# A transformer block on one Trainium2 core: LayerNorm 1 of all blocks by TensorE transposes, warm-up matmuls, early attention for block 0, and exact buffer dependencies

## The chip, the cores and the metric

The kernel runs on one core of a Trainium2 chip. The time is the device time of one execution, in microseconds (us). Before the change it is 264.82 us, the median of 3 runs (264.09 to 265.74).

Names used below, with what this kernel uses each for: TensorE (PE) does the matmuls, VectorE (DVE) and ScalarE (ACT) the elementwise work, GpSimd (POOL) elementwise work too, and SyncE (SP) issues DMA transfers. PSUM buffers hold matmul results until ACT or DVE takes ("evacuates") them to SBUF.

## The reference

One block of a diffusion-style transformer on x of 2048 tokens by 448 channels, in bfloat16: 16 heads of 28 channels, each token attending to itself and to 7 earlier tokens at distance 2, 4, ... 14; a gated MLP of width 1792. Six vectors (shift, scale and gate for each half) come from `silu(c) @ w_mod`.

```python
mod = (_silu(c) @ w_mod).reshape(1, 6, 1, -1)
sa, ca, ga, sb, cb, gb = (mod[:, i] for i in range(6))          # shortened
h = _layernorm(x) * (1 + ca) + sa                               # "LN1"
x = x + ga * attention(h, A_wqkv, A_wo)                         # window 8, dilation 2
h = _layernorm(x) * (1 + cb) + sb                               # "LN2"
gate = h @ W_gate; up = h @ W_up
x = x + gb * ((relu(gate) * up) @ W_down)
```

## The kernel before

The program handles the tokens in 4 blocks of 512 (each 4 tiles of 128) and attention in 18 tiles of up to 114 tokens. It lists all operations with what they read (`r`), what they write (`w`), a priority (`prio`, lower is earlier) and a guess of their cost. A list scheduler then fixes one order for each engine, so a priority or a dependency can move many instructions. A buffer in `w` means: wait for all earlier users of it.

The stages of block b: LN1 gives hT (normalized input, channels on partitions); the Q/K projections (`stage_qk`) and V projections (`stage_v`) read hT; attention tiles (logits, exp, mask, attention times V, division by the sum) give the attention output; the output projection `stage_y` adds it to x; LN2 gives h2T; then gate, up and down matmuls.

LN1 had two forms. Blocks 0 and 1 use TensorE transposes, blocks 2 and 3 DMA transposes with everything else on POOL:

```python
def stage_a_pe(b, prio, groups):
    ...                                             # statistics, 1/sigma
    pairs = [_Buf(poolF) for _ in range(2)]         # PSUM
    for j in range(4):
        hbuf = ln_normalize(..., DVE if b == 0 else POOL)
        ...  # 4 transposes of 128x128 into pairs
    for cc in range(4):
        ...  # evacuate to hT with scale (1+ca) and shift sa: ACT for cc < 2, else DVE

def stage_a_dma(b, prio):
    ...                                             # statistics, 1/sigma
    for t in range(4 * b, 4 * b + 4):
        hbuf = ln_normalize(t, rstd, nmr, 1, prio, POOL)
        ln_transpose(hbuf, ...)                     # DMA transpose into hT
    for cc in range(4):
        ln_affine(...)                              # POOL: hT * (1+ca) + sa, in place
```

Attention of one tile is in two halves that share the buffer `ea`. Both the exp and the mask list the whole of `ea` as written, so the second exp waits for the first mask:

```python
op(ACTE, _act(8 * nq), ex, r=[buf], w=[ea, (ea, half)], prio=eprio)
...
op(DVE, _dve(8 * nq, 0.52), mk, r=[(ea, half), mname], w=[ea, (ea, half, "m")], prio=eprio)
```

In the down-projection each token tile takes a token buffer `tok`, which the output addition also reads. The next tile's matmuls so wait for this tile's addition:

```python
op(PE, 7 * _mm(D), mm, r=..., w=[buf, tok], prio=prio, drain=PE_DRAIN)
...
op(DVE, 620, lambda e: e.tensor_tensor(o.at, buf.at[:, 0:D], x_sb[:, t, :], ALU.add),
   r=[buf, tok, ("x", t)], w=[o], prio=eprio)
```

The end of the program's listing, where the order is set:

```python
mod_cols((0, 1), "wmodA", 0, -5)
stage_a_pe(0, 0, ((0, 2), (2, 4)))
stage_qk(0, 50)
stage_a_pe(1, 30, ((0, 4),))
...                                  # Wg, Wu, Wd loads, issued from POOL, held back
stage_a_dma(2, 60)
stage_a_dma(3, 70)
...                                  # scalings of wo and Wd by the gates, on POOL
for t in range(NA):
    first = t < 5
    stage_attn(t, 200 + t if first else 500 + 10 * t, 140 + t if first else 500 + 10 * t)
    ...                              # stage_y at the same priorities, LN2 after each 4
```

The first priority of `stage_attn` is that of its TensorE work, the second that of ACT and DVE. The projections of block 1 have 150, those of blocks 2 and 3 have 300 and 400.

The softmax here doesn't subtract the row's maximum and nothing guards it: scores larger than these inputs give would overflow.

## Time and profile before

| | before |
|---|---|
| time, median of 3 (range) | 264.82 us (264.09 to 265.74) |
| span of the profiled execution | 262.4 us |
| TensorE busy | 229.6 us, 88% |
| POOL busy | 73.5 us, 28% |
| chain of waits | PE 76%, DVE 11%, POOL 6% |
| first gate matmul | 88.59 us |
| first gate matmul to the end | 173.8 us |

TensorE is the busiest engine and heads the chain of waits (the chain of work that ended last, followed back). The kernel's time is so its matmuls plus the stretches in which TensorE waits or runs slowly. The page of the kernel before, in 40 slices of 6.56 us, gives the busy share in tenths; PEclk is the granted TensorE clock in tenths of full speed:

```profile
PE   0589995468899799999999999999999999999784
...
POOL 7306907998924000013502215020130000000000
PEclk9999999558999999999999999999999999999999
```

The dip of PE in slices 7 to 9 comes with a POOL that is 70% to over 90% busy, and within it, in slices 8 and 9, the granted clock falls to a half. The same stretches with numbers, again for the kernel before (window, its length, PE busy with its instruction count, granted clock, DMA share, GB/s):

```profile
14.00:24.00 10.00, 9.69 (x36) 1.00 1.00 247
...
40.00:60.00 20.00, 10.95 (x138) 0.67 0.40 56
```

From 40 to 60 us TensorE loses 9 us, in part of the rest at half clock. The chain of waits of the kernel before tells why (start, duration, engine, tile and line):

```profile
51.89 2.97 POOL Wd L771 x3
54.87 3.89 POOL hT L510 x4
58.75 1.01 POOL Wd L771
60.05 1.11 PE psF L570 x3
```

L510 is `ln_affine`, L771 the scaling of Wd and L570 the Q/K projections. The projections wait for block 2's LN1, which stands in POOL's queue among other work. (They don't read Wd: the chain names its scaling last only because it ended just before them.)

Two other losses, from the timeline of the kernel before (start, duration, engine, line, operation, result and operands, shape, count, and in brackets the idle time before and what ended it). L597 is the V projection, L736 the down-projection:

```profile
14.09 1.67 PE L597 MATMUL psF<-Wv,hT 128*128 128x448 bf16 x4 [1.61 <-DVE hT L540]
15.98 4.37 PE L570 MATMUL psF<-hT,Wqk 128*128 128x512 bf16 x11 [0.22 <-DVE st L479]
...
88.59 0.81 PE L716 MATMUL psF<-h2T,Wg 128*128 128x512 bf16 x3 [0.16 <-issue]
...
252.77 2.82 PE L736 MATMUL psM<-Wd,bigR 128*128 128x448 bf16 x14 [0.72 <-DVE o_sb L743]
```

The first projections take 0.40 us per matmul, nearly twice what the same matmuls take later (0.22 us): they run "cold", at half rate, until 19.76 us. The recorded clock reads 1.00 from 14 to 24 us all the same, so here the durations decide. At the end, three down-projections (the last is shown) wait 0.72 us each for the output addition (L743). The first gate matmul (L716) at 88.59 us divides the kernel: from then on TensorE waits little, and from 160 to 240 us it is busy over 99%. In the same trace block 0's last output projection starts at 72.71 us, and block 0's h2T is complete at 85.19.

### The profile page before, as it was taken

To read this page: it belongs to the slowest core of one execution; us is meant where nothing else is said; L and a number is where in the kernel's file an instruction comes from. 1 tells how busy PE (TensorE), PEld (TensorE's weight loads), DVE (VectorE), ACT (ScalarE), POOL (GpSimd) and SP (SyncE) were. 2 spreads that over 40 slices of the span, in tenths; PEclk is the share of its full clock that TensorE was granted. 3 is DMA by queue.
4 is the path that set the end of the run, shared out by engine and by line. 5 is a ranking of instruction groups with operands and counts; after the bars stand their busy time and mean duration, and the time that the engine had idled before them with its cause. 6 is when DMAs were issued, how large, how long until landed. Compare 5 with 4: busy or idle time off the path is not lost.

```text
span 262.4 us, 4091 instructions
## 1 busy us (share of the span) xinstructions
PE 229.6 (88%) x1609; PEld 109.4 (42%) x1634; DVE 140.9 (54%) x277; ACT 120.2 (46%) x207; POOL 73.5 (28%) x98
## 2 busy tenths in 40 slices
PE   0589995468899799999999999999999999999784
PEld 0435542123344344444444444444444444444331
DVE  5986506667640377876867889633333433244311
ACT  2237777447547766677575656531113311123100
POOL 7306907998924000013502215020130000000000
PEclk9999999558999999999999999999999999999999
DMA  6996999001001000022002120002100001000011
GB/s 170 290 291 151 339 349 165 20 20 22 20 20 23 0 0 2 0 42 41 20 17 50 28 42 1 0 19 61 37 20 17 0 0 35 21 17 0 0 37 36
DMA packets 20924, 15.92 MB, mean 61 GB/s; under 512 B 13752, under 2 KB 19656, under 8 KB 20904
## 3 DMA queue, kind: packets, MB, share of 16 engines
q1 hardware_dynamic: 19736, 10.61, 17.3%
q0 software_dynamic: 896, 4.82, 5.3%
q8 instruction: 13, 0.21, 0.3%
q10 hardware_dynamic: 272, 0.23, 0.3%
q14 instruction: 7, 0.06, 0.1%
HBM read 10.67 MB, written 1.84 MB: 48 GB/s over the span
## 4 chain that ended last, share of the span: by engine, by line
PE 76%; DVE 11%; POOL 6%; issue 3%; ACT 2%
PE psF L716 36%; PE psM L736 16%; PE psF L570 11%; PE psF L597 4%; PE psM L681 3%; POOL Wd L771 3%; PE psL L624 3%; DVE EA L643 2%; PE psM L652 2%; DVE st L479 1%; POOL hT L510 1%; DVE o_sb L743 1%; ACT EA L638 1%; POOL wo_pad L768 1%; DVE qT L670 1%
## 5 line engine op out<-in xcount | busy, mean ns | idle before, releaser
L722 ACT ACTIVATE g_sb<-psF 128x512 bf16<-128x512 f32 x56 | 33.4, 597 | 67.3 <-PE psF L716 67.2
L724 DVE TENSOR_TENSOR bigR<-psF,g_sb 128x512 bf16<-128x512 f32 x56 | 38.7, 690 | 43.2 <-PE psF L716 39.4
L716 PE MATMUL psF<-h2T,Wu 128*128 128x512 bf16 x215 | 55.9, 379 | 0.8 <-issue 0.5
L716 PE MATMUL psF<-h2T,Wg 128*128 128x512 bf16 x213 | 55.7, 379 | 1.0 <-issue 0.6
L736 PE MATMUL psM<-Wd,bigR 128*128 128x448 bf16 x224 | 47.1, 353 | 3.6 <-DVE o_sb L743 2.6
L497 POOL TENSOR_SCALAR hb<-x_sb,rstd,nmr 128x448 bf16<-128x448 bf16 x28 | 22.4, 810 | 76.1 <-DVE nmr L490 64.0
L638 ACT ACTIVATE EA<-psL 128x912 bf16<-128x912 f32 (+1 forms) x36 | 33.2, 923 | 19.0 <-PE psL L624 16.4
L643 DVE TENSOR_TENSOR EA<-EA,maskA 128x912 bf16<-128x912 bf16 (+1 forms) x36 | 27.3, 758 | 18.5 <-ACT EA L638 18.3
L716 PEld LDWEIGHTS psF<-h2T,Wu 128*128 128x128 bf16 x224 | 21.3, 98 | 24.9
L736 PEld LDWEIGHTS psM<-Wd,bigR 128*128 128x128 bf16 x224 | 21.0, 98 | 25.6 <-DVE o_sb L743 4.0
L570 PE MATMUL psF<-hT,Wqk 128*128 128x512 bf16 x123 | 30.3, 400 | 0.8 <-POOL Wd L771 0.3
L716 PEld LDWEIGHTS psF<-h2T,Wg 128*128 128x128 bf16 x224 | 21.0, 98 | 23.8
L743 DVE TENSOR_TENSOR o_sb<-psM,x_sb 128x448 bf16<-128x448 f32 x16 | 10.0, 624 | 25.8 <-PE psM L736 25.6
L510 POOL TENSOR_SCALAR h2T<-h2T,modc 128x512 bf16<-128x512 bf16 (+1 forms) x16 | 13.7, 856 | 32.3 <-DMA h2T<-hb 31.1
L681 PE MATMUL psM<-wo_pad,qT 128*128 128x448 bf16 x64 | 16.3, 380 | 5.8 <-DVE qT L670 5.8
L479 DVE BATCH_NORM_STATS2 st<-x_sb 128x6 f32<-128x448 bf16 x32 | 19.6, 613 | 0.6
L570 PEld LDWEIGHTS psF<-hT,Wqk 128*128 128x128 bf16 x128 | 12.9, 103 | 16.3 <-issue 3.4
L624 PE MATMUL psL<-qT,kT 28*128 28x114 bf16 (+1 forms) x288 | 14.3, 220 | 4.7 <-ACT EA L638 4.6
L597 PE MATMUL psF<-Wv,hT 128*128 128x448 bf16 (+1 forms) x72 | 15.7, 365 | 1.6 <-DVE hT L540 1.6
L624 PEld LDWEIGHTS psL<-qT,kT 28*128 28x128 bf16 (+1 forms) x288 | 8.3, 98 | 16.9 <-ACT EA L638 7.4
L771 POOL TENSOR_TENSOR Wd<-Wd,gbc 128x448 bf16<-128x448 bf16 x14 | 14.6, 1067 | 0.0
L665 ACT ACTIVATE lnD<-psM 128x456 f32<-128x456 f32 x18 | 9.9, 550 | 7.6 <-PE psM L660 7.6
(70 smaller groups left out, 172.4 us busy)
## 6 DMA issues: line engine op xcount, KB each, us to landing
out_dram<-o_sb SPq DMA_DIRECT2D x16, 112.0 KB, 1.7
bigR<-in_w_mod_dram SPq DMA_DIRECT2D x1, 1568.0 KB, 15.6
Wd<-in_B_W_down_dram POOLq DMA_DIRECT2D x1, 1568.0 KB, 14.1
x_sb<-in_A_x_dram SPq DMA_DIRECT2D x3, 448.0 KB, 9.3
Wg<-in_B_W_gate_dram POOLq DMA_DIRECT2D x1, 1344.0 KB, 6.6
Wu<-in_B_W_up_dram POOLq DMA_DIRECT2D x1, 1344.0 KB, 10.0
bigR<-in_w_mod_dram SPq DMA_DIRECT2D x1, 784.0 KB, 7.5
bigR<-in_A_wqkv_dram SPq DMA_DIRECT2D x1, 672.0 KB, 8.9
```

Source lines behind the costliest of these rows:

```text
L497: f = lambda e: e.tensor_scalar(buf.at[:, 0:D], x_sb[:, t, :], rt[:, t:t + 1], nt[:, t:t + 1], ALU.mult, ALU.add)
L570: last = e.matmul(buf.at, Wqk[:, k, 512 * sec + 128 * g:512 * sec + 128 * g + 128], hT[:, k, KOFF + TB * b:KOFF + TB * b + TB], start=(k = ...
L597: last = e.matmul(buf.at[0:nk, 0:D], hT[:, k, KOFF + k0:KOFF + k0 + nk], Wv[:, k, :], start=(k == 0), stop=(k == 3))
L624: last = e.matmul(buf.at[0:nk, i, g * NQ:g * NQ + nq], kT[32 * r:32 * r + DH, g, KOFF + k0:KOFF + k0 + nk], qT[32 * r:32 * r + DH, g, s0:s ...
L638: return e.activation(dst, src, ACT.Exp)
L643: return e.tensor_tensor(d, d, msk[0:nk, None, 0:nq].to_broadcast([nk, 8, nq]), ALU.mult)
L681: last = e.matmul(buf.at[:, 0:D], qT[:, g, s0:s0 + 128], wo_pad[:, g, :], start=(g == 0), stop=(g == 3))
L716: last = e.matmul(buf.at, W[:, k, 128 * f:128 * f + 128], h2.at[:, k, :], start=(k == 0), stop=(k == 3))
L722: op(ACTE, _act(TB), lambda e, gs=gs, gb=bufs[0]: e.activation(gs.at, gb.at, ACT.Relu), r=[bufs[0]], w=[gs], prio=eprio)
L724: op(DVE, _dve(TB), lambda e, gs=gs, ub=bufs[1], f=f: e.tensor_tensor(hh.at[:, f, :], ub.at, gs.at, ALU.mult), r=[bufs[1], gs], w=[hh, (hh ...
L736: last = e.matmul(buf.at[:, 0:D], hh.at[:, f, 128 * j:128 * j + 128], Wd[:, f, :], start=(f == 0), stop=(f == NF - 1))
L771: op(POOL, 1000, lambda e, f=f: e.tensor_tensor(Wd[:, f, :], Wd[:, f, :], gbc[:, 1, :], ALU.mult), r=[("Wd", f), ("gbc", 1)], w=[("Wds", f ...
```

## The change

It has five intents: (1) take LN1 of blocks 2 and 3 from POOL and the DMA queue to TensorE transposes; (2) keep TensorE's clock up before the first real work by matmuls on zeros; (3) run attention of tiles 0 to 4 (block 0) among the projections of blocks 1 to 3, by TensorE priority 140 in place of 200; (4) drop the two superfluous waits shown above; (5) split and reorder loads, so that all weights are issued early from SP. The diff, cut to its core:

```diff
+        def keep_busy(n, prio, cost):
+            buf = _Buf(poolF)
+            ...   # n matmuls of warm[128x128] by warm[128x512]
+        op(DVE, 150, lambda e: e.memset(warm[:], 0.0), w=["warm"], prio=-30)
+        keep_busy(10, -30, 430)
+        keep_busy(16, -29, 217)
...
-        load(wmod[0:112, :, 0:2 * D], wmod_v[:, :, 0:2 * D], ["wmodA"], D * 2 * D * 2, -8)
+        load(wmod[0:112, 0:2, 0:2 * D], wmod_v[:, 0:2, 0:2 * D], ["wmodA0"], D * D * 2, -8)
+        load(wmod[0:112, 2:4, 0:2 * D], wmod_v[:, 2:4, 0:2 * D], ["wmodA1"], D * D * 2, -8)
...                # mod_cols: two halves, each after its half of the weights
+        for W, src, n in ((Wg, B_W_gate, "Wg"), (Wu, B_W_up, "Wu")):
+            load(...)                                  # from SP
+        load(Wd[:], ...)                               # from SP
...
-                op(ACTE, _act(8 * nq), ex, r=[buf], w=[ea, (ea, half)], prio=eprio)
+                op(ACTE, _act(8 * nq), ex, r=[buf] + ([ea] if half else []), w=[(ea, half)] + ([] if half else [ea]),
+                   prio=eprio)
...
-                op(DVE, ..., mk, r=[(ea, half), mname], w=[ea, (ea, half, "m")], prio=eprio)
+                op(DVE, ..., mk, r=[ea, (ea, half), mname], w=[(ea, half, "m")], prio=eprio)
...
-                   r=[buf, tok, ("x", t)], w=[o], prio=eprio)
+                   r=[buf, ("x", t)], w=[o], prio=eprio)
...
         stage_a_pe(0, 0, ((0, 2), (2, 4)))
+        keep_busy(5, 1, 217)
         stage_qk(0, 50)
         stage_a_pe(1, 30, ((0, 4),))
-        ...       # Wg, Wu, Wd loads from POOL
-        stage_a_dma(2, 60)
-        stage_a_dma(3, 70)
+        stage_a_pe(2, 60, ((0, 4),))
+        stage_a_pe(3, 70, ((0, 4),))
...
-            stage_attn(t, 200 + t if first else 500 + 10 * t, 140 + t if first else 500 + 10 * t)
+            stage_attn(t, 140 + t if first else 500 + 10 * t, 140 + t if first else 500 + 10 * t)
...                # stage_y likewise
```

The change also stops the scheduler from giving one buffer twice to one operation, and adds a DVE memset of hT's unused rows for blocks 2 and 3 (`hT1`). It also moves the second set of modulation vectors from priorities 230 to 232 to 136 to 139; makes the dependencies on h2T exact, like those on `ea`; and alters a few cost guesses.

More of the change, by code (lines that the diff above doesn't have):

```diff
@@ L114, in lat, with slot_for @@
             return self.XLAT
-        def slot_for(buf):
+        def slot_for(buf, taken=()):
             s = buf.slots
@@ L119, in slot_for @@
             for i, prev in enumerate(s.last):
+                if (id(s), i) in taken:
+                    continue
                 if prev is None:
@@ L135, in schedule @@
                 bad = False
+                taken = set()
                 for b in o["allocs"]:
-                    s = slot_for(b)
+                    s = slot_for(b, taken)
                     if s is None:
@@ L140, in schedule @@
                         break
+                    taken.add((id(b.slots), s[1]))
                     slot_t = max(slot_t, s[0])
@@ L333, in bass_adaLN_cond__sliding_local_dilated__glu_gated_reglu__prompt_kernel @@
         nmr2 = sb("nmr2", [128, NT], F32)
+        warm = sb("warm", [128, 512], BF16)
         crow = sb("crow", [112, 4], BF16)
@@ L373, in bass_adaLN_cond__sliding_local_dilated__glu_gated_reglu__prompt_kernel @@
         op(DVE, 350, lambda e: e.memset(hT[64:128, 3, KOFF:KOFF + 2 * TB], 0.0), w=["hT0"], prio=-14)
+        op(DVE, 350, lambda e: e.memset(hT[64:128, 3, KOFF + 2 * TB:KOFF + S], 0.0), w=["hT1"], prio=26)
         op(DVE, 350, lambda e: e.memset(Wqk[64:128, 3, :], 0.0), w=["wqkz"], prio=-14)
@@ L394, in bass_adaLN_cond__sliding_local_dilated__glu_gated_reglu__prompt_kernel, with mm @@
            r=["Bsel"], w=["Bsel"], prio=-8)
+        def keep_busy(n, prio, cost):
+            buf = _Buf(poolF)
+            def mm(e):
+                last = None
+                for _ in range(n):
+                    last = e.matmul(buf.at, warm[:, 0:128], warm[:, 0:512], start=True, stop=True)
+                return last
+            op(PE, n * cost, mm, r=["warm"], w=[buf], prio=prio, drain=PE_DRAIN)
+        op(DVE, 150, lambda e: e.memset(warm[:], 0.0), w=["warm"], prio=-30)
+        keep_busy(10, -30, 430)
+        keep_busy(16, -29, 217)
         def load(dst, src, w, nbytes, prio, r=(), eng=SP, issue=450.0):
@@ L408, in bass_adaLN_cond__sliding_local_dilated__glu_gated_reglu__prompt_kernel @@
         load_x(2, 4, -9, eng=ACTE)
-        load(wmod[0:112, :, 0:2 * D], wmod_v[:, :, 0:2 * D], ["wmodA"], D * 2 * D * 2, -8)
+        load(wmod[0:112, 0:2, 0:2 * D], wmod_v[:, 0:2, 0:2 * D], ["wmodA0"], D * D * 2, -8)
+        load(wmod[0:112, 2:4, 0:2 * D], wmod_v[:, 2:4, 0:2 * D], ["wmodA1"], D * D * 2, -8)
+        load(Wv[:, 0:3, :], A_wqkv[0:384, 2 * D:3 * D].rearrange("(k p) n -> p k n", p=128),
+             [("wv", k) for k in range(3)], 384 * D * 2, -7)
+        load(Wv[0:64, 3, :], A_wqkv[384:448, 2 * D:3 * D], [("wv", 3)], 64 * D * 2, -7)
         load(Wraw[:, 0:3, :], A_wqkv[0:384, 0:2 * D].rearrange("(k p) n -> p k n", p=128),
@@ L412, in bass_adaLN_cond__sliding_local_dilated__glu_gated_reglu__prompt_kernel @@
         load(Wraw[0:64, 3, :], A_wqkv[384:448, 0:2 * D], [("wraw", 3)], 64 * 2 * D * 2, -7)
-        load(Wv[:, 0:3, :], A_wqkv[0:384, 2 * D:3 * D].rearrange("(k p) n -> p k n", p=128),
-             [("wv", k) for k in range(3)], 384 * D * 2, -7)
-        load(Wv[0:64, 3, :], A_wqkv[384:448, 2 * D:3 * D], [("wv", 3)], 64 * D * 2, -7)
         load_x(4, 8, -6)
         load_x(8, 12, -5)
-        load_x(12, 16, -5)
-        load(wmod[0:112, :, 2 * D:6 * D], wmod_v[:, :, 2 * D:6 * D], ["wmodB"], D * 4 * D * 2, -4)
+        load(wmod[0:112, 0:2, 2 * D:6 * D], wmod_v[:, 0:2, 2 * D:6 * D], ["wmodB0"], D * 2 * D * 2, -4)
+        load(wmod[0:112, 2:4, 2 * D:6 * D], wmod_v[:, 2:4, 2 * D:6 * D], ["wmodB1"], D * 2 * D * 2, -4)
+        load_x(12, 16, -4)
         for r in range(4):
@@ L422, in bass_adaLN_cond__sliding_local_dilated__glu_gated_reglu__prompt_kernel @@
                  [("wo", r)], 4 * DH * D * 2, -3, r=["wo0"])
+        for W, src, n in ((Wg, B_W_gate, "Wg"), (Wu, B_W_up, "Wu")):
+            load(W[:, 0:3, :], src[0:384, :].rearrange("(k p) n -> p k n", p=128), [n + "a"], 384 * FF * 2, -2)
+            load(W[0:64, 3, :], src[384:448, :], [n + "b"], 64 * FF * 2, -2)
+        load(Wd[:], B_W_down.rearrange("(f p) n -> p f n", p=128), [("Wd", f) for f in range(NF)], FF * D * 2, -1)
         op(POOL, 900, lambda e: e.memset(Wqk_h[:, :, :, DH:32], 0.0), r=["wqkz"], w=["wqk0"], prio=-16)
@@ L441, in mod_cols, with mm @@
             buf = _Buf(poolM)
-            def mm(e):
+            def mm(e, ks):
                 last = None
-                first = True
-                for vi, vec in enumerate(vecs):
+                for k in ks:
                     for cc in range(4):
-                        for k in range(4):
+                        for vi, vec in enumerate(vecs):
                             M = ROWS[cc]
@@ L451, in mm @@
                                             wmod[0:112, k, D * vec + 128 * cc:D * vec + 128 * cc + M],
-                                            silu[:, k:k + 1], start=first, stop=(vi == 1 and cc == 3 and k == 3),
+                                            silu[:, k:k + 1], start=(k == 0 and cc == 0 and vi == 0),
+                                            stop=(k == 3 and cc == 3 and vi == 1),
                                             skip_group_check=True)
-                            first = False
                 return last
             op(DVE, 70, lambda e: e.memset(buf.at[:, 0:8], 0.0), w=[buf], prio=prio - 20)
-            op(PE, 2400, mm, r=[wname, "silu"], w=[buf], prio=prio, drain=PE_DRAIN)
-            op(DVE, 150, lambda e: e.tensor_copy(modc[:, col:col + 4], buf.at[:, 0:4]), r=[buf, "eps"],
+            for i in range(2):
+                op(PE, 750, lambda e, i=i: mm(e, (2 * i, 2 * i + 1)), r=[wname + str(i), "silu"], w=[buf], prio=prio,
+                   drain=PE_DRAIN)
+            op(DVE, 80, lambda e: e.tensor_copy(modc[:, col:col + 4], buf.at[:, 0:4]), r=[buf, "eps"],
                w=[("mod", col)], prio=prio)
@@ L471, in mm @@
                 return last
-            op(PE, 4 * _mm(D), mm, r=["wmodB", "silu_bc"], w=[buf], prio=prio, drain=PE_DRAIN)
+            op(PE, 4 * _mm(D), mm, r=["wmodB0", "wmodB1", "silu_bc"], w=[buf], prio=prio, drain=PE_DRAIN)
             op(((ACTE, _act(D), lambda e: e.activation(gbc[:, i, :], buf.at[:, 0:D], ACT.Copy)),
@@ L485, in ln_rstd @@
             ts = range(t0, t1)
-            op(ACTE, 290, lambda e: e.activation(lt[:, t0:t1], mvt[:, t0:t1, 1], ACT.Ln, bias=eps_col[:, 0:1]),
+            op(ACTE, 300, lambda e: e.activation(lt[:, t0:t1], mvt[:, t0:t1, 1], ACT.Ln, bias=eps_col[:, 0:1]),
                r=[(tag, "mv", t) for t in ts] + ["eps"], w=[(tag, "ln", t0)], prio=prio)
@@ L493, in ln_rstd, with ln_normalize @@
                w=[(tag, "nmr", t) for t in ts], prio=prio)
-        def ln_normalize(t, rt, nt, tag, prio, eng):
+        def ln_normalize(t, rt, nt, tag, prio, eng, extra=()):
             buf = _Buf(hb_slots)
@@ L498, in ln_normalize, with ln_transpose @@
                                           ALU.mult, ALU.add)
-            op(eng, 390 if eng == DVE else 620, f, r=[("x", t), (tag, "rstd", t), (tag, "nmr", t)], w=[buf],
+            op(eng, 390 if eng == DVE else 720, f, r=[("x", t), (tag, "rstd", t), (tag, "nmr", t)], w=[buf] + list(extra),
                prio=prio)
             return buf
-        def ln_transpose(buf, dst, w, prio):
-            op(SP, 0, lambda e: e.dma_start_transpose(dst(), buf.at), r=[buf], w=w, prio=prio, dma=450000,
+        def ln_transpose(buf, dst, r, w, prio):
+            op(SP, 0, lambda e: e.dma_start_transpose(dst(), buf.at), r=[buf] + r, w=w, prio=prio, dma=20000,
                issue=1250.0)
@@ L511, in f @@
                                        modc[0:rows, col + cc:col + cc + 1], ALU.mult, ALU.add)
-            op(POOL, 700, f, r=deps + [("mod", col), ("mod", col + 4)], w=w, prio=prio)
+            op(POOL, 850, f, r=deps + [("mod", col), ("mod", col + 4)], w=w, prio=prio)
         def stage_a_pe(b, prio, groups):
@@ L540, in stage_a_pe @@
                 fd = lambda e, src=src, dst=dst, sc=sc, bi=bi: e.tensor_scalar(dst, src(), sc, bi, ALU.mult, ALU.add)
-                op(*((ACTE, 720, fa) if cc < 2 else (DVE, 700, fd)), r=pairs[cc // 2:cc // 2 + 1] + [("mod", 0), ("mod", 4), "hT0"],
+                op(*((ACTE, 720, fa) if cc < 2 else (DVE, 700, fd)), r=pairs[cc // 2:cc // 2 + 1] + [("mod", 0), ("mod", 4)],
                    w=[("hT", b, cc)], prio=prio)
-        def stage_a_dma(b, prio):
-            for t in range(4 * b, 4 * b + 4):
-                ln_stats(t, st, mv, 1, prio)
-            ln_rstd(4 * b, 4 * b + 4, mv, lnv, rstd, nmr, 1, prio)
-            for t in range(4 * b, 4 * b + 4):
-                hbuf = ln_normalize(t, rstd, nmr, 1, prio, POOL)
-                c0 = KOFF + 128 * t
-                ln_transpose(hbuf, lambda c0=c0: hT[:, :, c0:c0 + 128], [("hTr", t)], prio)
-            for cc in range(4):
-                R = ROWS[cc]
-                ln_affine(lambda cc=cc, R=R, b=b: hT[0:R, cc, KOFF + TB * b:KOFF + TB * b + TB],
-                          [("hTr", t) for t in range(4 * b, 4 * b + 4)], [("hT", b, cc)], 0, R, cc, prio)
         qscale = float(DH) ** -0.5
@@ L572, in mm @@
                         return last
-                    op(PE, 4 * _mm(TB), mm, r=[("wqk", k, sec) for k in range(4)] + ["wqkz", "hT0"] + hT_deps(TB * b, TB * b + TB),
+                    op(PE, 4 * _mm(TB), mm, r=[("wqk", k, sec) for k in range(4)] + ["wqkz", "hT0"] + (["hT1"] if b > 1 else []) + hT_deps(TB * b, TB * b + TB),
                        w=[buf], prio=prio, drain=PE_DRAIN)
@@ L599, in mm @@
                 return last
-            op(PE, 4 * _mm(D), mm, r=[("wv", k) for k in range(4)] + ["wvz", "hT0"] + hT_deps(k0, k0 + nk) + (["hTpad"] if t == 0 else []),
+            op(PE, 4 * _mm(D), mm, r=[("wv", k) for k in range(4)] + ["wvz", "hT0"] + (["hT1"] if k0 + nk > 2 * TB else []) + hT_deps(k0, k0 + nk) + (["hTpad"] if t == 0 else []),
                w=[buf], prio=prio, drain=PE_DRAIN)
@@ L643, in mk @@
                     return e.tensor_tensor(d, d, msk[0:nk, None, 0:nq].to_broadcast([nk, 8, nq]), ALU.mult)
-                op(DVE, _dve(8 * nq, 0.52), mk, r=[(ea, half), mname], w=[ea, (ea, half, "m")], prio=eprio)
+                op(DVE, _dve(8 * nq, 0.52), mk, r=[ea, (ea, half), mname], w=[(ea, half, "m")], prio=eprio)
             ob = _Buf(poolM)
@@ L693, in stage_ln2 @@
                 for j in (j0, j0 + 1):
-                    hbuf = ln_normalize(j, rstd2, nmr2, 2, prio, POOL)
+                    hbuf = ln_normalize(j, rstd2, nmr2, 2, prio, POOL, [h2] if j == 4 * b else [])
                     c0 = 128 * (j - 4 * b)
-                    ln_transpose(hbuf, lambda c0=c0: h2.at[:, :, c0:c0 + 128], [h2, (h2, "r", j)], prio)
+                    ln_transpose(hbuf, lambda c0=c0: h2.at[:, :, c0:c0 + 128], [h2], [(h2, "r", j)], prio)
             for cc in range(4):
                 R = ROWS[cc]
-                ln_affine(lambda cc=cc, R=R: h2.at[0:R, cc, :], [(h2, "r", j) for j in range(4 * b, 4 * b + 4)],
-                          [h2, (h2, cc)], 8, R, cc, prio)
+                ln_affine(lambda cc=cc, R=R: h2.at[0:R, cc, :], [h2] + [(h2, "r", j) for j in range(4 * b, 4 * b + 4)],
+                          [(h2, cc)], 8, R, cc, prio)
             return h2
@@ L705, in stage_gu @@
             hh = _Buf(hh_slots)
-            extra = ["wmodA", "wmodB"] + [("wraw", k) for k in range(4)]
+            extra = ["wmodA0", "wmodA1", "wmodB0", "wmodB1"] + [("wraw", k) for k in range(4)]
             for f in range(NF):
@@ L750, in bass_adaLN_cond__sliding_local_dilated__glu_gated_reglu__prompt_kernel @@
         stage_a_pe(0, 0, ((0, 2), (2, 4)))
+        keep_busy(5, 1, 217)
         stage_qk(0, 50)
         stage_a_pe(1, 30, ((0, 4),))
-        hold = [("x", 12), (1, "nmr", 7)]
-        load(Wg[:, 0:3, :], B_W_gate[0:384, :].rearrange("(k p) n -> p k n", p=128), ["Wga"], 384 * FF * 2, 45,
-             eng=POOL, issue=1100.0, r=hold)
-        load(Wg[0:64, 3, :], B_W_gate[384:448, :], ["Wgb"], 64 * FF * 2, 45, eng=POOL, issue=1100.0, r=hold)
-        load(Wu[:, 0:3, :], B_W_up[0:384, :].rearrange("(k p) n -> p k n", p=128), ["Wua"], 384 * FF * 2, 45,
-             eng=POOL, issue=1100.0, r=hold)
-        load(Wu[0:64, 3, :], B_W_up[384:448, :], ["Wub"], 64 * FF * 2, 45, eng=POOL, issue=1100.0, r=hold)
-        load(Wd[:], B_W_down.rearrange("(f p) n -> p f n", p=128), [("Wd", f) for f in range(NF)], FF * D * 2, 46,
-             eng=POOL, issue=1100.0, r=hold)
-        stage_a_dma(2, 60)
-        stage_a_dma(3, 70)
-        mod_cols((3, 4), "wmodB", 8, 230)
-        mod_row(0, 2, 231)
-        mod_row(1, 5, 232)
+        stage_a_pe(2, 60, ((0, 4),))
+        stage_a_pe(3, 70, ((0, 4),))
+        mod_cols((3, 4), "wmodB", 8, 138)
+        mod_row(0, 2, 136)
+        mod_row(1, 5, 139)
         for g in range(4):
@@ L790, in bass_adaLN_cond__sliding_local_dilated__glu_gated_reglu__prompt_kernel @@
             first = t < 5
-            stage_attn(t, 200 + t if first else 500 + 10 * t, 140 + t if first else 500 + 10 * t)
+            stage_attn(t, 140 + t if first else 500 + 10 * t, 140 + t if first else 500 + 10 * t)
             end = sum(span(t)[:2])
             while done_y < NT and 128 * (done_y + 1) <= end:
-                p = 200 + t if first else 500 + 10 * t
+                p = 140 + t if first else 500 + 10 * t
                 ep = 140 + t if first else 500 + 10 * t
```

## The prediction

> **What bounds the kernel now.** TensorE is busy 88% of 262.4 us (busy table) and heads the chain of waits (76%). From 90 us to the end it is nearly saturated: 19.9 of 20 us per stretch from 160 to 240 us (table of stretches). The losses are early. (a) Nothing useful runs on TensorE before 9.16 us, when the first modulation weights land. (b) Its first dense matmuls run cold: 0.43 us per 512-column matmul at 15 to 19.7 us against 0.216 later (timeline). (c) From 40 to 60 us it is busy 4.5 and 6.5 us of 10, and the granted clock falls to 0.85 and 0.50: projections of block 2 wait for its LN1, which goes POOL normalize, DMA transpose (6.3 us to landing), POOL affine (3.9 us for four), with wo and Wd scalings between them on POOL (chain of waits). (d) From 70 to 90 us it loses 3 us. (e) At the end each of three down-projections waits 0.72 us for the previous output add.
>
> **What the change does.**
> - LN1 of blocks 2 and 3: 32 TensorE transposes (0.4 us per four matmuls, 3 to 4 us in all) and 8 evacuations (ACT 0.72, DVE 0.53) replace 8 DMA transposes and 8 POOL affines (7.3 us of POOL).
> - Weight loads leave POOL (3.9 us of issue) for the SP queue and start earlier; at the 290 to 340 GB/s shown, Wd lands at 36 to 39 us, as before.
> - 26 warm-up matmuls before 9 us cost nothing, TensorE being idle; five more cost at most 1 us at 11 us. First projections at 0.22 us: up to 2.5 us gained. [...]
> - DVE memsets ahead of the modulation columns keep the first block's hT at about 14 us.
> - Block-0 attention goes among the projections of blocks 1 to 3, covering its latencies.
> - Exact dependencies: the second exp no longer waits for the first mask (about 1 us); the down-projection no longer waits for the output add: 3 x 0.72 = 2.2 us, fully on the chain.
>
> **Sum.** Replaying TensorE's new order by hand with measured durations: block 0 projections end near 24 us, then about 48 us of work up to the last V projection, near 75 us if dense, against 86.5 now. ACT has about 33 us of work in that stretch and DVE 30; masks and products slow down (0.63 to 1.3 us) while POOL scales Wd. I add 3 to 5 us of stalls: 78 to 80 us; the first gate matmul, which also needs LN2 of block 0 (about 11 us after its last projection), near 80 against 88.4. Gain 8.5. With 1 from the exp chain and 2.2 at the end: 264.8 - 11.7 = 253 us.
>
> **What would show it.** No half-clock slice at 50 to 60 us; 512-column projections at 0.22 us from the first; first gate matmul at 77 to 82 us; no wait of a down-projection on the output add; the stretch from first gate matmul to end shrinks from 174 to about 171 us.
>
> **What would make it wrong.** Better: ACT and DVE keep up, gate starts near 75. Worse: ACT in-order waits (LN1 evacuations ahead of exps, psF slots shared by transposes and projections) leave TensorE idle over 7 us, or modulation weights land late because weight loads crowd the queue; or POOL's Wd scaling delays LN2 of block 0, so the gate start hardly moves.
>
> Chances: faster by over 2% 0.90, within 2% 0.08, slower 0.02. Predicted 253.0 us, range 247.5 to 258.5.

(That warm-up matmuls would bring the first projections to 0.22 us was my estimate: the trace of the kernel before shows only the two rates, 0.43 and 0.216 us.)

## The result, and the profile after

The changed kernel takes 250.37 us, the median of 3 runs (249.91 to 251.38). All outputs are right. The ratio to the kernel before is 0.946, 95% interval 0.939 to 0.953: faster by 14.45 us in the medians, where 11.7 was predicted. Ratios in this document are the mean time of one kernel's fast runs over the mean of the other's fast runs of the same rounds, so they are not quite the ratios of the medians.

| | before | after | after, control run |
|---|---|---|---|
| time, median | 264.82 us | 250.37 us | 250.51 us |
| span of the profiled execution | 262.4 us | 249.6 us | 247.9 us |
| mean granted clock in it | 0.973 | 0.986 | 0.993 |
| TensorE busy | 88% | 94% | |
| POOL busy | 28% | 25% | |
| chain of waits, PE / DVE / POOL | 76 / 11 / 6% | 89 / 6 / not listed | |
| first gate matmul | 88.59 us | 79.32 us | 77.73 us |
| first gate matmul to the end | 173.8 us | 170.3 us | 170.2 us |

The profiled execution of the changed kernel is its slowest of the three. The control run (first experiment) is the same program again. In the latter, the gain in span is 10.9 us before the first gate matmul and 3.6 us after it, together 14.5 us, as in the medians. The split is not clean: before its first gate matmul the changed kernel has done the attention times V of one more tile (six against five).

The page of the changed kernel, busy tenths in 40 slices:

```profile
PE   8879999999995999999999999999999999999894
...
PEclk9989999999998899999999999999999999999999
```

Slices 7 to 9 are full now; one slice of 5 has come in at 75 to 81 us. The changed kernel in the windows used before:

```profile
14.00:24.00 10.00, 8.39 (x46) 0.97 1.07 231
24.00:40.00 16.00, 15.76 (x170) 1.00 1.05 292
40.00:60.00 20.00, 18.93 (x177) 1.00 0.03 11
60.00:74.00 14.00, 13.95 (x85) 1.00 0.16 32
74.00:80.00 6.00, 2.98 (x54) 0.96 0.08 16
80.00:90.00 10.00, 9.84 (x89) 0.85 0.01 2
```

From 40 to 60 us TensorE is busy 18.93 us in place of 10.95, at full clock. The waits of 74 to 80 us are seen in TensorE's timeline of the changed kernel (L638 logits, L667 attention times V, L731 gate and up, L696 output projection):

```profile
67.24 0.92 PE L696 MATMUL psM<-wo_pad,qT 128*128 128x448 bf16 x4
...
70.59 3.95 PE L611 MATMUL psF<-Wv,hT 128*128 128x448 bf16 x20
74.47 0.37 PE L638 MATMUL psL<-qT,kT 28*128 28x114 bf16 x8
75.99 0.37 PE L638 MATMUL psL<-qT,kT 28*128 28x114 bf16 x8 [1.15 <-ACT EA L652]
77.39 0.37 PE L638 MATMUL psL<-qT,kT 28*128 28x114 bf16 x8 [1.03 <-ACT EA L652]
78.44 0.39 PE L667 MATMUL psM<-EA,vaug 128*32 128x114 bf16 x16 [0.68 <-DVE EA L658]
...
79.32 1.28 PE L731 MATMUL psF<-h2T,Wg 128*128 128x512 bf16 x3 [0.16 <-issue]
...
80.78 1.91 PE L731 MATMUL psF<-h2T,Wu 128*128 128x512 bf16 x4
```

The projections end at 74.5 us. What follows is attention of tiles 5 and 6, whose logits wait for exps, until LN2 of block 0 is ready. Block 0's last output projection is at 67.24 us, and POOL's timeline of the changed kernel shows the last step of its LN2, L537:

```profile
42.90 14.34 POOL L778 TENSOR_TENSOR Wd<-Wd,gbc 128x448 bf16<-128x448 bf16 x12 [5.17 <-DMA Wd<-in_B_W_down_dram]
...
75.18 3.84 POOL L537 TENSOR_SCALAR h2T<-h2T,modc 128x512 bf16<-128x512 bf16 x4 [3.21 <-DMA h2T<-hb]
```

h2T is complete at 79.02 us and the gate matmuls begin 0.30 us later. Then the clock falls: the four `Wu` matmuls at 80.78 take 0.48 us each. In the 6 us before (74 to 80) TensorE was busy 2.98 us, with no single gap over 1.15 us. The granted clock by microsecond, in the changed kernel (columns as in the windows above):

```profile
12.00:13.00 1.00, 1.00 (x3) 0.50 1.09 354
...
80.00:81.00 1.00, 1.00 (x4) 0.50 0.00 0
```

The start and the end, from the timeline of the changed kernel (L409 warm-up, L475 modulation columns, L556 transposes, L611 V projection, L751 down-projection):

```profile
8.39 0.83 PE L475 MATMUL psM<-silu,bigR 112*128 112x1 bf16 x16
...
11.79 1.91 PE L409 MATMUL psF<-warm 128*128 128x512 bf16 x4 [0.22 <-issue]
13.49 1.06 PE L556 MATMUL psF<-ident,hb 128*128 128x128 bf16 x8
16.14 2.43 PE L611 MATMUL psF<-Wv,hT 128*128 128x448 bf16 x12 [1.58 <-DVE Wqk L452]
...
235.17 10.77 PE L751 MATMUL psM<-Wd,bigR 128*128 128x448 bf16 x56 [0.79 <-DVE bigR L739]
```

The down-projection of the last block is one run of 56 matmuls without a wait: the three gaps of 0.72 us are gone. At the start the projections run at full rate (12 in 2.43 us), but begin at 16.14 us, against 14.09 before: the clock had fallen again, to 0.50 at 12 us (after one-column matmuls, transposes and gaps only, from 8.4 to 11.6 us; no run separates the three), and the five late warm-up matmuls (the record of one is missing) ran at half rate ahead of the last transposes.

### The profile page after: what moved, and what is told of

The parts are those of the page before. It is cut to its first block, busy times and chain, and to the rows that moved or that the text cites. A ratio compares the mean times of both kernels' runs of the same rounds, so it can differ in the third digit from the quotient of the medians.

```text
span 249.6 us, 4195 instructions
## 1 busy us (share of the span) xinstructions
PE 235.1 (94%) x1671; PEld 113.6 (46%) x1697; DVE 143.5 (57%) x289; ACT 118.9 (48%) x205; POOL 63.4 (25%) x85
## 4 chain that ended last, share of the span: by engine, by line
PE 89%; DVE 6%; issue 2%; ACT 2%
PE psF L731 39%; PE psM L751 17%; PE psF L584 10%; PE psF L611 6%; PE psM L696 5%; PE psL L638 4%; PE psM L667 2%; PE psF L556 2%; PE psM L675 1%; ACT EA L652 1%; DVE EA L658 1%; DVE st L506 1%; PE psM L475 1%; PE psF L409 1%; PE psM L496 1%
## 5 line engine op out<-in xcount | busy, mean ns | idle before, releaser
L731 PE MATMUL psF<-h2T,Wu 128*128 128x512 bf16 x216 | 57.0, 384 | 0.9 <-issue 0.6
L731 PE MATMUL psF<-h2T,Wg 128*128 128x512 bf16 x213 | 55.7, 382 | 1.1 <-issue 0.8
L751 PE MATMUL psM<-Wd,bigR 128*128 128x448 bf16 x224 | 46.5, 353 | 0.8 <-DVE bigR L739 0.8
L524 POOL TENSOR_SCALAR hb<-x_sb,rstd,nmr 128x448 bf16<-128x448 bf16 x28 | 21.6, 783 | 84.0 <-DVE nmr L517 75.9
L731 PEld LDWEIGHTS psF<-h2T,Wu 128*128 128x128 bf16 x224 | 21.7, 99 | 25.8 <-issue 1.1
L658 DVE TENSOR_TENSOR EA<-EA,maskA 128x912 bf16<-128x912 bf16 (+1 forms) x36 | 25.7, 716 | 11.2 <-ACT EA L652 10.9
L751 PEld LDWEIGHTS psM<-Wd,bigR 128*128 128x128 bf16 x224 | 21.4, 98 | 22.0 <-DVE bigR L739 1.3
L731 PEld LDWEIGHTS psF<-h2T,Wg 128*128 128x128 bf16 x224 | 20.7, 98 | 23.5
L584 PE MATMUL psF<-hT,Wqk 128*128 128x512 bf16 x122 | 29.3, 380 | 0.6 <-issue 0.5
L537 POOL TENSOR_SCALAR h2T<-h2T,modc 128x512 bf16<-128x512 bf16 (+1 forms) x16 | 14.4, 914 | 18.3 <-DMA h2T<-hb 18.3
L778 POOL TENSOR_TENSOR Wd<-Wd,gbc 128x448 bf16<-128x448 bf16 x14 | 16.4, 1203 | 5.2 <-DMA Wd<-in_B_W_down_dram 5.2
L584 PEld LDWEIGHTS psF<-hT,Wqk 128*128 128x128 bf16 x128 | 11.6, 98 | 12.7
L611 PE MATMUL psF<-Wv,hT 128*128 128x448 bf16 (+1 forms) x72 | 15.0, 353 | 1.6 <-DVE Wqk L452 1.6
L638 PE MATMUL psL<-qT,kT 28*128 28x114 bf16 (+1 forms) x288 | 13.5, 212 | 2.2 <-ACT EA L652 2.2
L696 PE MATMUL psM<-wo_pad,qT 128*128 128x448 bf16 x64 | 14.7, 353 | 0.7 <-DVE qT L685 0.7
L638 PEld LDWEIGHTS psL<-qT,kT 28*128 28x128 bf16 (+1 forms) x288 | 7.8, 95 | 12.9 <-issue 3.8
```

The lines of the kernel that those rows point to most:

```text
L524: f = lambda e: e.tensor_scalar(buf.at[:, 0:D], x_sb[:, t, :], rt[:, t:t + 1], nt[:, t:t + 1], ALU.mult, ALU.add)
L584: last = e.matmul(buf.at, Wqk[:, k, 512 * sec + 128 * g:512 * sec + 128 * g + 128], hT[:, k, KOFF + TB * b:KOFF + TB * b + TB], start=(k = ...
L611: last = e.matmul(buf.at[0:nk, 0:D], hT[:, k, KOFF + k0:KOFF + k0 + nk], Wv[:, k, :], start=(k == 0), stop=(k == 3))
L638: last = e.matmul(buf.at[0:nk, i, g * NQ:g * NQ + nq], kT[32 * r:32 * r + DH, g, KOFF + k0:KOFF + k0 + nk], qT[32 * r:32 * r + DH, g, s0:s ...
L658: return e.tensor_tensor(d, d, msk[0:nk, None, 0:nq].to_broadcast([nk, 8, nq]), ALU.mult)
L696: last = e.matmul(buf.at[:, 0:D], qT[:, g, s0:s0 + 128], wo_pad[:, g, :], start=(g == 0), stop=(g == 3))
```

## The experiments

Theory: the gain is LN1 and the early attention together (the gate starts earlier), with about 1 us from the exp chain, 2.2 us from the end, and 2 to 2.5 us from the warm-up. Rivals: the early attention alone does it, or LN1 alone; the warm-up is worth little; the place of the weight loads is what counts. Experiments of one call ran on one chip and shared the runs of the kernel before. There were three calls, with medians of before of 265.3, 265.74 and 265.33 us.

| run | undoes or adds | median, us (range) | ratio to before (95%) |
|---|---|---|---|
| c_after | nothing (control) | 250.51 (249.44–252.49) | 0.9437 (0.9393–0.9482) |
| e3_no_warm | all warm-up matmuls out | 251.34 (250.55–252.83) | 0.9456 (0.9416–0.9496) |
| e3b_no_five | the five late ones out | 253.97 (252.99–255.22) | 0.9563 (0.9523–0.9603) |
| e4_tok_back | down-projection waits again | 253.02 (252.32–253.99) | 0.9530 (0.9491–0.9568) |
| e1_dma_ln1 | LN1 of blocks 2, 3 by DMA again | 256.31, three of four slow | none |
| e2_late_attn | attention back to priority 200 | 254.35 (253.42–255.63) | 0.9563 (0.9519–0.9607) |
| e5_pe_ln1_only | before, plus LN1 by TensorE | 260.57 (260.24–261.31) | 0.9807 (0.9777–0.9838) |
| e6_ea_back | exp and mask share `ea` again | 251.51 (250.56–253.07) | 0.9466 (0.9432–0.9501) |
| e7_pool_loads | weight loads on POOL, held back | 251.00 (250.34–251.56) | 0.9463 (0.9434–0.9492) |
| b1_fill_gap | attention of tiles 5 to 7 early too | 246.95 (246.13–248.71) | 0.9315 (0.9282–0.9348) |
| b2_start | warm-ups and two memsets moved | 246.89 (246.82–247.45) | 0.9311 (0.9282–0.9341) |
| b3_both | b1 and b2 | 244.26 (244.07–244.79) | 0.9210 (0.9180–0.9239) |

Not all expectations printed below were met. Within or close to their ranges were c_after, e4, e6, e7, and the totals of e2 and b1, whose gate came later than foretold (87.21 us for 81 to 84, 82.11 for about 79). e3 lies at the edge of its first range (0.8 us), e3b in that of its rival B, but with a changed order. e5 missed both of its ranges. b2 and b3 came out faster than foretold. e1 is not counted.

### The control

> The changed kernel again, as the control for the three runs beside it: 250.4 us, within 1 us.

The same program as the changed kernel: 250.51 us over 6 runs. Runs of it spread over 3 us, and the start shows one reason. TensorE's timeline of the control, to be set beside that of the changed kernel above:

```profile
11.65 1.03 PE L409 MATMUL psF<-warm 128*128 128x512 bf16 x4
12.52 0.61 PE L556 MATMUL psF<-ident,hb 128*128 128x128 bf16 x8
14.73 2.43 PE L611 MATMUL psF<-Wv,hT 128*128 128x448 bf16 x12 [1.60 <-DVE Wqk L452]
```

Here the clock stayed up (1.00 from 8 to 18 us), the warm-up matmuls took 0.26 us each in place of 0.48, the eight transposes 0.61 us in place of 1.06 at half clock, and the first projection began 1.41 us earlier. The two executions differ before that: their 26 early warm-up matmuls start alike at 1.19 us, but by their durations run at half rate until 4.5 us in the changed kernel's first profile and until 6.6 in the control, so that they end at 8.6 and 9.6 us. The later end leaves a shorter stretch before the late ones (9.6 to 11.65 us, against 8.6 to 11.79); what makes the two executions differ is not shown. A comparison with the control is therefore blurred by 1 to 2 us, the spread that the start alone brings (1.41 us at the first projection, 1.59 at the gate).

### Warm-up matmuls: e3_no_warm and e3b_no_five

```diff
-        op(DVE, 150, lambda e: e.memset(warm[:], 0.0), w=["warm"], prio=-30)
-        keep_busy(10, -30, 430)
-        keep_busy(16, -29, 217)
...
-        keep_busy(5, 1, 217)
```

(e3b takes out only the last line.)

> All 31 warm-up matmuls removed. Theory (read from the trace of after): the warm-ups give nothing net, because the clock falls back before the first projection, the five late ones run at half rate and hold the first block's last two transposes up by 2 us; so within 0.8 us of after, first projection 2 us earlier (near 14 us instead of 16.1)[...]. Rival (my prediction): the warm-ups are worth 2 to 2.5 us, so 252.5 to 253 us.

> Only the five late warm-ups removed, the 26 early ones kept. Theory: first projection near 14.6 us but at half rate, since the 26 end at 8.6 us and the clock falls; total within 0.8 us of after. Rival A: the 26 alone keep the array warm, so the 2 us hold-up is saved and the total is about 248.5 us. Rival B: the five are what brings the gain, so 252 us or more.

Without any warm-up the time is 251.34 us, 0.8 us over the control, with overlapping intervals: their net worth is about 0.8 us and not told from zero, below the 2 to 2.5 us of the prediction. The timeline of the kernel without warm-ups shows both sides of it:

```profile
13.76 4.64 PE L608 MATMUL psF<-Wv,hT 128*128 128x448 bf16 x12 [1.92 <-ACT hT L563]
```

The projections run cold (at half rate), 12 in 4.64 us, but begin at 13.76 us, earlier than with warm-ups (14.73 and 16.14). The 12 are done at 18.40 us, against 17.16 in the control and 18.57 in the changed kernel's first profile. The half rate saved and the delay added nearly cancel.

Without the five late ones the time rises by 3.5 us, which is no clean measure of the five. The timeline of that kernel has two lines out of place:

```profile
14.69 4.41 PE L611 MATMUL psF<-Wv,hT 128*128 128x448 bf16 x12 [2.74 <-ACT hT L566]
...
82.97 1.49 PE L731 MATMUL psF<-h2T,Wg 128*128 128x512 bf16 x3 [0.47 <-POOL h2T L537]
```

The projections run cold although 26 warm-up matmuls came before. But the scheduler, which plans with costs, also set the last output projection of block 0 from 67.24 to 70.71 us, so that LN2 and the gate came later (82.97). Most of the 3.5 us may be this other order. The experiment changed two things and settles neither.

### The wait at the end: e4_tok_back

```diff
-                   r=[buf, ("x", t)], w=[o], prio=eprio)
+                   r=[buf, tok, ("x", t)], w=[o], prio=eprio)
```

> The output add holds the down-projection's token again, all else as in after. Theory: three gaps of 0.72 us come back between the last four down-projections, 2.2 us in all, so 252.6 us; the start of the gate matmuls stays near 79 us. Rival: the add's latency is hidden by something else and the end is bound by output DMA, so within 0.7 us of after.

2.5 us over the control, and the timeline of this kernel has the gaps back (the last of three):

```profile
244.23 2.82 PE L751 MATMUL psM<-Wd,bigR 128*128 128x448 bf16 x14 [0.72 <-DVE o_sb L758]
```

Its first gate matmul is at 77.82 us, 0.09 us from the control's. So the difference is at the end, and 3 x 0.72 = 2.16 us of it is seen. This term of the prediction is shown.

### LN1 and early attention: e1_dma_ln1, e2_late_attn, e5_pe_ln1_only

```diff
 e1, on after:      -stage_a_pe(2, ...); stage_a_pe(3, ...)    +stage_a_dma(2, 60); stage_a_dma(3, 70)
 e2, on after:      -stage_attn(t, 140 + t if first ...)       +stage_attn(t, 200 + t if first ...)   (stage_y likewise)
 e5, on before:     -stage_a_dma(2, 60); stage_a_dma(3, 70)    +stage_a_pe(2, ...); stage_a_pe(3, ...)
```

> LN1 of blocks 2 and 3 back on POOL and DMA transposes, all else as in after (the scheduler then puts the whole block-0 attention before the projections of block 2). Theory: the LN1 path is the main term, so TensorE idles again between 40 and 60 us, the first gate matmul starts at 86 us or later against 77.7 to 79.3, and the total is 256 to 260 us. Rival: the early attention is what fills the gap, LN1's path hardly matters: within 2.5 us of after.

> Block-0 attention and its output projections at before's later priority on TensorE, all else as in after (the last tile's padding columns are computed too, which costs nothing, so that no logarithm of an unwritten column is taken). Theory: early attention is the smaller term; the projections are dense, but the last output projection of block 0 comes later and LN2 of block 0 with it, so first gate matmul at 81 to 84 us, total 252.5 to 256 us. Rival: attention's place is the main term: 257 us or more. Second rival: nothing, within 1 us of after.

> The kernel before with nothing but LN1 of blocks 2 and 3 on TensorE (and the slot fix in the scheduler and the last tile's padding, without which it does not schedule or check). Theory: this alone takes out the stall of 40 to 60 us: gate start at 80 to 84 us, half-clock slices gone, total 256 to 259 us, that is 6 to 9 us of the 14.8. Rival: on its own it gains under 3 us, since attention then exposes its own chain.

In the last, shorter attention tile the matmuls write 110 of 114 columns per group, and the logarithm then read what the buffer held before; another order had given it other contents. The runs compute all 114 columns there, which changes no result (in the trace of the changed kernel these matmuls take 215 ns with 110 columns and 221 with 114, on the mean). (e5 also has the change's fix of the scheduler's double buffers.)

e1 is inconclusive. Three of its four runs, the profiled one among them, count as slow; the only fast run took 252.21 us, 1.8 over the control, which lies within what the rival foretold (early attention fills the gap, under 2.5 us). It was run at another time. No ratio was formed. (The slow profile has the stall back, 13.15 us busy of 20 from 40 to 60, but a slow run can't carry the argument.) e5 asks the same question from the other side.

e5 adds only LN1 by TensorE to the kernel before and gains 5.2 us, not the whole (ratio 0.981: clear of noise, but "unclear" by the 2% rule). I had expected 6 to 9 us, with the gate at 80 to 84. Its windows (columns as above) show where it gained and where it gave back:

```profile
40.00:60.00 20.00, 19.77 (x185) 1.00 0.01 3
...
74.00:80.00 6.00, 3.14 (x52) 0.74 0.21 44
80.00:90.00 10.00, 5.66 (x46) 0.50 0.01 2
```

The stall of 40 to 60 us is gone (19.77 of 20 busy), and the projections end at 74.4 us, 12.2 us earlier than before. But block 0's last output projection and LN2 have hardly moved: h2T is complete at 84.14 us, against 85.19. Until then, and 6 us beyond, attention of tiles 5 to 7 stands alone in TensorE's order: its chain of exp, mask, sum and division keeps TensorE waiting (busy 5.66 us of 10 from 80 to 90 us), and the clock halves (0.50 there). Of e5's timeline, the last output projection of block 0, the last step of its LN2 and the first gate matmul:

```profile
71.19 0.92 PE L686 MATMUL psM<-wo_pad,qT 128*128 128x448 bf16 x4
...
80.27 3.87 POOL L515 TENSOR_SCALAR h2T<-h2T,modc 128x512 bf16<-128x512 bf16 x4 [4.35 <-DMA h2T<-hb]
...
90.34 1.89 PE L721 MATMUL psF<-h2T,Wg 128*128 128x512 bf16 x4
```

The gate begins at 90.34 us, no earlier than the 88.59 before (attention times V of seven tiles is done ahead of it in place of five, which is why the time still falls). e2, the changed kernel without the early attention, has a like picture in its timeline:

```profile
73.53 0.93 PE L696 MATMUL psM<-wo_pad,qT 128*128 128x448 bf16 x4
...
82.80 3.51 POOL L537 TENSOR_SCALAR h2T<-h2T,modc 128x512 bf16<-128x512 bf16 x4 [4.16 <-DMA h2T<-hb]
...
87.21 1.89 PE L731 MATMUL psF<-h2T,Wg 128*128 128x512 bf16 x4
```

and loses 3.8 us of the gain. In the changed kernel that output projection is at 67.24 us, 6.3 earlier, h2T is complete 7.3 us earlier and the gate begins 7.9 us earlier. So LN1 alone is not enough, and the early attention brings block 0's LN2 and the gate forward. That this is its whole effect is not shown: from 74 to 90 us the two also differ in the mean clock, 0.57 in e2 and 0.89 in the changed kernel. The rival "early attention alone" is not excluded, since e1's runs don't settle it, but e5 shows that LN1 alone takes away the stall and gives 5.2 us.

### The exp chain and the place of the loads: e6_ea_back, e7_pool_loads

```diff
 e6: -  exp  r=[buf] + ([ea] if half else []), w=[(ea, half)] + ([] if half else [ea]);  mask r=[ea, (ea, half), mname], w=[(ea, half, "m")]
     +  exp  r=[buf], w=[ea, (ea, half)];                                                mask r=[(ea, half), mname],     w=[ea, (ea, half, "m")]
 e7: -  Wg, Wu, Wd loads from SP at priority -2 and -1
     +  the same loads from POOL, held back until x tile 12 and LN1 statistics of block 1, as before
```

> The second exp of a tile waits for the first mask again, and the second mask for the first, all else as in after. Theory: about 1 us is lost, where the exps gate TensorE at 74 to 79 us and while attention fills the early stages: 250.8 to 252.5 us. Rival: under 0.5 us, as TensorE has other work wherever exps run.

> The three MLP weights loaded from POOL and held back as before, all else as in after. Theory: the place of these loads is worth little, the POOL issue (about 4 us) delays block 2's normalize by 3 us and with it the scalings: 250 to 252.5 us. Rival: crowding the SP queue early costs time in after, so 249.5 us or less.

e6 takes 251.51 us, 1.0 over the control, with overlapping intervals: inconclusive. It was run at another time. Its profile can be paired with the changed kernel's first one, since both begin their projections late (16.15 and 16.14 us): there the gate comes 0.93 us later and the span is 1.0 us longer, which speaks for about 1 us, but from one pair. e7 takes 251.00 us, 0.5 over it, overlapping too; its profile, with the same late start (15.97 us), is 0.6 us shorter than the changed kernel's, so that not even the sign is known. The place of the loads is worth little.

### Filling the gap: b1_fill_gap, b2_start, b3_both

The windows after the change leave two losses: 3.0 us idle at 74 to 80 us, with half clock after it, and the start. b1 gives three more tiles to the early attention, b2 orders the start, b3 does both.

```diff
 b1: -            first = t < 5
     +            first = t < 8          (and all 114 columns in the last tile)
 b2: - memsets of hT1 and Wu's unused rows at once, on DVE
     + the same, after block 0's hT is done
     - keep_busy(5, 1, 217)
     + keep_busy(4, 1, 217, after the last transpose of block 0)
     + 3 warm-up matmuls after the first half of the modulation columns
```

> after, with attention tiles 5 to 7 given the early priority as well, so that they interleave with the projections of block 3. Theory: after still has TensorE idle for about 3 us between 72.9 and 77.7 us (tile 5's exps and LN2 of block 0 in front of the first gate matmul), and the clock drops behind it, which costs 2 us more at 78 to 81 us. Filled: no clock drop at 80 us, first gate matmul near 79 us but with 6 us more work done before it; total 246 to 248.5 us. Rival: the extra attention only delays the last output projection of block 0 and LN2 with it, 250 us or more.

> after, with the 5 late warm-ups replaced by 3 ahead of the first transpose and 4 behind the last one, and two memsets moved behind the first block's evacuation. Theory: the first projection comes at 13.5 to 14.5 us at full rate (16.1 and 14.7 in the two traces of after), which carries to the gate start, so 1 to 2.5 us less than after: 248 to 249.5 us. Rival: the first block is then bound by its weights' landing or by ACT, no gain, within 0.7 us of after.

> Both edits. If they add up: 244.5 to 247.5 us. If the earlier start only lengthens the wait for LN2 of block 0: as b1_fill_gap.

Against the control, b1 gains 3.6 us, b2 3.6, both 6.25. They were run at other times. b2's timeline shows the start and the gate:

```profile
13.95 2.44 PE L617 MATMUL psF<-Wv,hT 128*128 128x448 bf16 x12 [0.68 <-ACT hT L572]
...
74.01 1.04 PE L737 MATMUL psF<-h2T,Wg 128*128 128x512 bf16 x4 [0.17 <-POOL h2T L543]
```

The projections begin at 13.95 us and at full rate. All four of its runs had a granted clock of 1.00 and lie within 0.7 us, where the control's spread over 3. b2 moves warm-ups and memsets together, so its 3.6 us is not divided between them. Nor is it the start alone: against the control's profile the projections begin 0.8 us earlier but the gate 3.7, with the logits of one tile less ahead of it. The windows of b3:

```profile
14.00:24.00 10.00, 10.00 (x58) 1.00 1.07 240
...
74.00:80.00 6.00, 6.00 (x52) 1.00 0.07 14
80.00:90.00 10.00, 10.00 (x102) 1.00 0.10 20
```

Both losses are gone. b3's first gate matmul is at 78.01 us, later than b2's: it is no loss, since more attention is done by then (attention times V of eight tiles, against five in b2). At 244.26 us b3 beats both kernels: 0.921 of before, and 0.9210 / 0.9437 = 0.976 of the changed one.

## Why the prediction was right

The prediction of 253.0 us (range 247.5 to 258.5, faster) held, with 250.37 measured, and the two main terms worked as predicted: LN1 by TensorE took the stall away, and an earlier LN2 of block 0 brought the gate forward. Two smaller terms are off or unsettled, and the gate's place is in part luck. Point by point:

- **The stall of 40 to 60 us.** Right: the half-clock slice is gone and 10.95 us busy became 18.93. e5 shows that LN1 by TensorE alone does this.
- **The gate start near 80 us, gain 8.5.** Right: 79.32 us in the first profile, 77.73 in the control, so 9.3 to 10.9 us. It came about by a somewhat different sum. I added 3 to 5 us of stalls spread over the projections. From 24 to 74 us TensorE idled only 1.36 us (0.24 + 1.07 + 0.05), and the last V projection ended at 74.5, my "near 75 if dense". The 3 us were lost after it, from 74 to 80 us, where I had named the cause (LN2 of block 0, about 11 us after its last projection: 67.24 + 0.92 to 79.02 is 10.9 us) but not that TensorE would find so little else to do. That 3 us lost here made up for 3 to 5 us foretold elsewhere was luck.
- **The end, 2.2 us.** Right, and shown by e4: gaps of 0.72 us away in after, back in e4, 2.5 us. The stretch from gate to end shrank by 3.5 us (3.2 foretold), but one attention tile has also moved out of it, so this sum confirms no more than e4 does.
- **The exp chain, 1 us.** Not settled: e6's medians give 1.0 us with overlapping intervals, its profile 1.0 us in one pair of like starts. In the changed kernel the logits of tiles 5 and 6 still wait 1.15 and 1.03 us for exps.
- **The warm-up, "First projections at 0.22 us: up to 2.5 us gained".** This term was mis-sized. The rate came out as said, but the projections began at 16.14 or 14.73 us, later than the 14.09 before, and e3 puts the net gain at 0.8 us. "Cost nothing" is not borne out: in e3, without the 26, the first modulation matmuls run at 7.52 us, when the 26 were still running in both profiles of the changed kernel; and e3b, with the 26 but not the five, begins its projections at 14.69 us, 0.9 later than e3. The five late ones, at half rate in one execution, held up the last transposes. The half rate that the prediction puts "at 15 to 19.7 us" lasts 5.7 us for the projections of before (14.09 to 19.76), and 3.3 and 5.4 us for the warm-ups in the two profiles of the changed kernel: no one length. "DVE memsets ahead of the modulation columns keep the first block's hT at about 14 us": the evacuation into hT began at 14.59 us in the first profile, where it waited for the transposes, and at 13.18 in the control; so the memsets did not set it.
- **Weight loads.** Wd landed at 42.9 us, not 36 to 39; by e7 the place of the loads matters little.
- **Masks that slow down beside POOL.** Right: the median of all 36 masks is 0.63 us, and four of the six that start between 42 and 56 us, about while POOL scales Wd (42.90 to 57.24 us), took 0.86 to 1.28 us. The two fall together in time; no run shows that POOL is the cause.

The rest of the difference, 11.7 us foretold and 14.45 measured: in the first pair of profiles the span shrank by 12.8 us, 9.3 at the gate (8.5 foretold) and 3.5 after it (3.2 foretold). That profile is the changed kernel's slowest run, 1.0 us over its median; in the control the two parts are 10.9 and 3.6. So most of it is the gate start, whose gain was underestimated by 0.8 to 2.4 us, and it varies by 1.6 us between executions of one program.

The terms tried one at a time are 5.2 (LN1 added to before, e5, against before) and, each against the control, 3.8 (e2), 2.5 (e4), 1.0 (e6), 0.8 (e3) and 0.5 (e7): 13.8 us together, of the 14.8 us between the control and before. They need not add up: some are not told from zero, and LN1 and early attention lean on each other.

Open: the worth of early attention without LN1 (e1 is inconclusive), the five late warm-ups by themselves (e3b changed the order too), whether the exp chain is worth its 1 us, and the earlier modulation vectors and the exact h2T dependencies, which no run undoes.

## What to carry to other kernels

A stall taken away upstream pays only as far as the next join (where two chains of work meet) moves too: with LN1 alone the projections ended 12.2 us earlier and the kernel gained 5.2, since LN2 of block 0 ended only 1.1 us earlier. Look for the latency-bound chain before a join, start it early among independent matmuls, and keep later independent work at hand to fill what is left (3.6 us in b1, for one changed number and a padded last tile). Warm-up matmuls are not free because TensorE is idle: see that none stands before the first real work at half rate (in the changed kernel the late ones took 0.48 us each and the projections began at 16.14 us, in the control 0.26 and 14.73), that no cold gap follows them (in e3b, with the 26 alone, the first 12 projections still took 0.37 us each), and that small memsets on another engine don't hold up the chain to the first matmul (in e3 two memsets, of 0.81 and 0.48 us, let DVE start its half of hT 0.8 us after ACT).
